# One array of expert rows, one array of attention outputs, and the weight splits on GpSimd

## The chip, the core and the metric

The kernel runs on one core of a Trainium2 chip. The metric is device time in microseconds (us): the median over several executions. One execution was also recorded by the hardware profiler; all rows below come from that one. TensorE is called PE here (its weight loads PEld), VectorE DVE, ScalarE ACT, GpSimd POOL, and SyncE SP, which only issues DMAs.

## The reference

Attention, then a mixture of experts with a skip, then a rational feed-forward layer, all in float32:

```
scores = z @ z.T / S                          # B=8, S=3072, dq=64
x = (u * (relu(scores)**2 @ v)).reshape(24576, 256)
do = x @ w_skip > 0                           # the other tokens keep x
e = argmax(x[do] @ w_gate); g = softmax weight of e     # 8 experts
x[do] += g * (relu(x[do] @ w1[e]) @ w2[e])    # 256 -> 1024 -> 256
h = x @ w_in                                  # 256 -> 2048
P = a0 + a1 h + a2 h^2 + a3 h^3
Q = 1 + |b0| |h| + |b1| h^2
out = (P / (Q + 1e-6)) @ w_out                # 2048 -> 256
```

A float32 matrix is multiplied as a rounded high part and the low rest (`wp` and its second half, `ah` and `al`, `mgh` and `mgl`), so every weight, value and activation has to be split once: a cast makes the high part and a subtraction the low one.

## The kernel before, in words

**Rows, ticks and segments.** The 24576 tokens are 96 attention rows of 256 tokens, 12 rows to a batch. A row is 12 ticks, one for each 256 keys: PE makes the scores `S` of a tick from the transposed keys `T1`, `T4`; ACT and DVE make `ah` and `al` of them; PE adds them times the values `V` into `accA`. Every batch needs its own `T1`, `T4` and `V`, made from loads of `z` and `v` about when the batch begins (the first batch ends with tick 143). The rows are cut into seven segments of 16, 14, 14, 14, 14, 12 and 12 rows (`SEGS`).

**The route of a row** (`r0` to `r21`). When `accA` is complete, DVE multiplies it with `u`, which was loaded into the buffer `xs` (`r0`, L747). SP stores the result into the array of attention outputs (`r21`, L767). PE, ACT, DVE and POOL find expert and gate weight and count the token's place among those of its expert (`r1` to `r14`), POOL turns that into row numbers (`r15`), and POOL scatters 2 x 128 token rows to the 256 slots of their expert in the segment's array `xs{g}` (`r16`, L889), and their numbers into an overflow list `ov` (L895) for tokens that find no slot. Buffer `xs` has two copies, so the load of `u` for row r+2 (L645) waits for the scatters of row r.

**Lag rows.** In all but the last segment, the last `2*LAGT[g]` rows (4, 4, 4, 4, 4, 2) lag: a token of theirs that finds no slot in its own segment may go to the next segment's slots. Since each segment has its array, such a row issues two more scatters (L882, into `xs{g+1}`), and its token number is stored in a mirrored form (`NOTOK`, `MIRROR`), so that the expert stage can tell to which of two output arrays a token belongs.

**The expert stage (MoE1)** of a segment loads 8 tiles of 256 slots (`mr<-xs`, L1191), multiplies them with the expert's weights, four units to a tile (`h`, L1137; `accM`, L1156), and scatters the results back over the attention outputs, `x2_{g}`. In segments 0 to 5 this is four scatters a tile: two of the tokens that belong to `x2_{g}`, two of those of `x2_{g+1}` (`scatter`, L1234). Row numbers out of bounds are dropped. The empty slots were filled with default rows by DMAs of SP (`prefill`, L1418).

**The last layer (MoE2)** then loads the attention outputs of the segment (`mr<-x`, L1191) in tiles of two rows, and its units (`h` at L1148, `accM` at L1166) run mixed with the attention ticks of the next segment.

**Weight preparation.** The expert weights come as raw chunks; the first four are split at their first use, the other 28 by `plan_w1prep`: SP loads two raw halves into `wr` (four buffers), a cast of each half goes into `wp` on ACT, DVE or POOL, a subtraction on DVE or POOL gives the low half, and SP stores the tile to `wsc1`. These chunks are spread over 160 ticks from tick 16. The MoE2 weights are decoded by `plan_w2prep`, nine DVE instructions (L354 to L362) for each half.

**What sets the order.** A planner (`Flow`) is given every piece of work with a wished time and, for each engine that may do it, a duration: "A.52|D.335s|G.588" means ACT at 0.52 us, DVE at 0.335 us or POOL at 0.588 us. It places the pieces one after the other, and the order in which it places them is the program order of each engine's queue. Each engine runs its queue strictly in order. Two DMAs whose declared regions of one DRAM array overlap wait for each other, even where the rows they write differ.

## Time and profile before

| | |
|---|---|
| median of 3 runs | 5580.26 us (5570.92 to 5585.91) |
| the profiled execution | 5576.21 us |
| its span, first to last instruction | 5574.5 us |
| granted TensorE clock, mean over the span | 0.987 |
| busy: PE / PEld / DVE / ACT / POOL | 95% / 90% / 81% / 76% / 58% |

The span begins with attention alone (segment 0, to about 530 us), has the first expert stage to about 690 us, then MoE2 mixed with attention, broken by six more expert stages, to about 5000 us, and MoE2 alone at the end. A time in brackets at the end of a row of the trace is how long the engine had been idle before the instruction, and what it waited for.

### The profile page before, as it was taken

What the parts mean: (1) busy time and instruction counts of PE and PEld (TensorE: products, weight loads), DVE (VectorE), ACT (ScalarE), POOL (GpSimd) and SP (SyncE); (2) the same over time, 40 slices, a digit from 0 to 9 for tenths busy, and PEclk for the clock granted to TensorE, in tenths of its full rate; (3) what the DMA queues carried; (4) which work ended last, traced back from release to release, by engine and by line L of the source; (5) the groups of instructions that cost most, each with busy time, mean ns of one, the idle gap of its engine ahead of it and who ended that gap; (6) DMA issues with size and microseconds to landing.
All of it is one profiled execution on the core that took longest, in us unless ns stands there. A gap on an engine that the chain in (4) does not pass through costs nothing.

```text
span 5574.5 us, 108436 instructions
## 1 busy us (share of the span) xinstructions
PE 5300.9 (95%) x39885; PEld 5026.1 (90%) x39885; DVE 4502.0 (81%) x7499; ACT 4233.4 (76%) x7737; POOL 3259.4 (58%) x4835
## 2 busy tenths in 40 slices
PE   8988899999999999999999999999999999999888
PEld 8988799999999998999999999999998989989777
DVE  6764288884999975999957999949999679986998
ACT  8875388884888874888856888848888668876998
POOL 3434356653655654656545656536566456665998
PEclk9999999999999999999999999999999999999999
DMA  5554521027210046100163101271011540026000
GB/s 191 197 174 145 218 66 56 25 87 258 79 34 29 27 154 233 42 28 23 49 238 139 33 22 59 80 266 55 24 45 39 194 160 29 26 87 211 16 24 17
DMA packets 224816, 540.29 MB, mean 97 GB/s; under 512 B 36978, under 2 KB 136321, under 8 KB 187666
## 3 DMA queue, kind: packets, MB, share of 16 engines
q1 hardware_dynamic: 188754, 448.71, 23.2%
q0 software_dynamic: 35520, 84.56, 4.4%
q8 instruction: 316, 5.18, 0.4%
q14 instruction: 226, 1.85, 0.1%
HBM read 413.38 MB, written 167.41 MB: 104 GB/s over the span
## 4 chain that ended last, share of the span: by engine, by line
PE 61%; DVE 16%; ACT 7%; POOL 6%; issue 6%; DMA 4%; SPq 0%; POOLq 0%; DVEq 0%; ACTq 0%
PE accA L686 21%; PE h L1148 11%; PE accM L1166 11%; PE h L1137 4%; PE accM L1156 4%; PE S L663 3%; PE S L664 3%; DVE mp L1354 2%; DVE h L1355 2%; DVE mq L1369 2%; DVE mgh L1368 2%; DVE al L678 1%; DVE mq L1371 1%; PE lp L777 1%; DMA x<-mo,mti 1%
## 5 line engine op out<-in xcount | busy, mean ns | idle before, releaser
L686 PE MATMUL accA<-V,ah 128*128 128x256 f32 x9216 | 1286.1, 283 | 43.5 <-DVE xs L747 22.3
L1148 PE MATMUL h<-mx,W 128*128 128x512 f32 x4608 | 1212.4, 399 | 43.6 <-DVE mgl L1364 22.3
L686 PEld LDWEIGHTS accA<-V,ah 128*128 128x128 f32 x9216 | 1177.5, 190 | 60.8 <-ACT ah L414 23.9
L410 POOL TENSOR_TENSOR mgl<-mq,mu 128x512 fp32r<-128x512 f32 x496 | 666.5, 1345 | 667.6 <-DVE mq L1371 378.7
L1148 PEld LDWEIGHTS h<-mx,W 128*128 128x128 f32 x4608 | 816.8, 189 | 191.5 <-DVE mgl L1364 26.7
L678 DVE TENSOR_TENSOR al<-S,ah 128x512 fp32r<-128x512 f32 x1152 | 788.2, 685 | 230.4 <-ACT ah L414 198.2
L1166 PE MATMUL accM<-W,mgh 128*128 128x256 f32 x6144 | 849.0, 281 | 19.7 <-DVE mgh L1368 16.9
L667 ACT ACTIVATE S<-S 128x512 f32<-128x512 f32 x1152 | 679.0, 589 | 206.6 <-PE S L664 196.9
L1166 PEld LDWEIGHTS accM<-W,mgh 128*128 128x128 f32 x6144 | 780.7, 189 | 28.7 <-DVE mgh L1368 19.9
L686 PE MATMUL accA<-V,al 128*128 128x256 f32 x4608 | 737.7, 283 | 16.7 <-DVE al L678 16.3
L670 ACT ACTIVATE S<-S 128x512 f32<-128x512 f32 x1152 | 673.7, 585 | 25.0
L1348 POOL TENSOR_SCALAR mq<-mu,coef 128x512 f32<-128x512 f32 x524 | 435.3, 831 | 421.1 <-ACT mu L1341 416.0
L1341 ACT ACTIVATE mu<-h 128x512 f32<-128x512 f32 x768 | 457.7, 596 | 275.2 <-PE h L1148 258.5
L414 ACT ACTIVATE ah<-S 128x512 fp32r<-128x512 f32 x958 | 572.6, 598 | 103.1 <-PE accA L686 72.1
L686 PEld LDWEIGHTS accA<-V,al 128*128 128x128 f32 x4608 | 626.4, 190 | 25.3 <-DVE al L678 21.3
L1354 DVE TENSOR_TENSOR mp<-mp,h 128x512 f32<-128x512 f32 x768 | 521.8, 681 | 122.1 <-ACT mp L1342 113.6
L1342 ACT ACTIVATE mp<-h,coef 128x512 f32<-128x512 f32 x768 | 596.0, 776 | 1.9 <-DVE h L1355 1.6
L664 PE MATMUL S<-T,T 128*128 128x256 f32 x2304 | 591.3, 281 | 0.6 <-ACT T L607 0.4
L1355 DVE SCALAR_TENSOR_TENSOR h<-mp,coef,h 128x512 f32<-128x512 f32 x768 | 573.9, 748 | 3.7
L410 POOL TENSOR_TENSOR mq<-mq,mu 128x512 f32<-128x512 f32 x394 | 520.3, 1322 | 35.0 <-DVE mq L1348 9.4
L1166 PE MATMUL accM<-W,mgl 128*128 128x256 f32 x3072 | 497.4, 284 | 31.4 <-DVE mgl L1364 23.6
L663 PE MATMUL S<-T,T 128*128 128x256 f32 x1920 | 502.1, 286 | 21.6 <-ACT T L588 12.5
(188 smaller groups left out, 9910.0 us busy)
## 6 DMA issues: line engine op xcount, KB each, us to landing
W<-wsc SPq DMA_DIRECT2D x184, 1024.0 KB, 6.2
W<-wsc POOLq DMA_DIRECT2D x48, 1024.0 KB, 5.3
Wv<-wsc SPq DMA_DIRECT2D x64, 512.0 KB, 6.0
vr<-in_v_dram SPq DMA_DIRECT2D x96, 256.0 KB, 2.9
wsc<-wp SPq DMA_DIRECT2D x24, 1024.0 KB, 5.0
xs<-in_u_dram SPq DMA_DIRECT2D x96, 256.0 KB, 2.8
x<-xs SPq DMA_DIRECT2D x96, 256.0 KB, 2.2
mr<-x SPq DMA_DIRECT2D x96, 256.0 KB, 3.3
```

Source lines behind the costliest of these rows:

```text
L410: (nc.vector if e == "D" else nc.gpsimd).tensor_tensor(*a, **k)
L663: mm(o, lhsT=lw, rhs=rw, start=(jj == 0), stop=False, skip_group_check=True)
L664: mm(o, lhsT=lw, rhs=T4[b, ic], start=False, stop=(jj == 1), skip_group_check=True)
L667: act(st["s"], st["s"], AF.Relu, scale=1.0 / S)
L670: act(st["s"], st["s"], AF.Square)
L678: ttt(st["lo"], st["s"], st["hi"].bitcast(F32), op=ALU.subtract)
L686: mm(accs[b, ic][:, it * TT : (it + 1) * TT], lhsT=a[:, jj * TT + it * P : jj * TT + (it + 1) * P], rhs=VV[b, jp][:, vi, jj * D : (jj + 1) ...
L1148: mm(h, lhsT=lw, rhs=rw, start=(k == 0 and i == 0), stop=(k == NK - 1 and i == 2), skip_group_check=True)
L1166: mm(accs_[it // 2][:, it % 2 * TT : (it % 2 + 1) * TT], lhsT=(gh, gl)[part][:, it * P : (it + 1) * P], rhs=w[i][:, 512 + ff * D : 512 + ( ...
L1342: pt("p1", "A.664", ["l1b"], lambda: act(buf("mp"), s["h"], AF.Identity, scale=a3, bias=a2), ["mp"])
L1354: pt("p2", "D.602", ["p1", "abs"], lambda: ttt(s["p"], s["p"], s["h"], op=ALU.mult))
L1355: pt("p3", "D.663", ["p2", "abs"], lambda: stt(s["h"], s["p"], a1, s["h"], op0=ALU.add, op1=ALU.mult), (), ["mp"])
```

## The change

Three things change together. **The arrays:** the seven `xs{g}` become one array with the segments in falling order, and the seven `x2_{g}` one array with the rows in falling order of row pairs. A scatter may write everything below the end of its own segment (`xs[0:xs_end(g)]`, `x2[0:end]`), so it reaches the next segment as well, and the index alone says which: a lag row issues no L882 scatters, an MoE1 tile issues two scatters for four, and the mirrored numbers go. The route's small POOL and DVE instructions of a lag row become fewer (13 to 11 in `r13`, 4 to 2 in `r14`, 7 to 4 in `r15`); those of another row become one more (3 to 4 in `r15`). **The weight splits:** in `plan_w1prep` the subtraction may run on POOL alone, and the cast on POOL or DVE. **The spread:** the 28 chunks are planned over 110 ticks (16 to 126) in place of 160 (16 to 176). Over the whole program the arithmetic on PE is the same; POOL issues 44 scatters into `xs` and 96 into `x2` fewer, and makes 48 weight subtractions (9 before) and 31 weight casts (13 before); DVE makes none of its 39 subtractions and 17 casts (21 before); ACT makes none of its 14 casts. The loop for tokens that overflowed even the next segment gathers from one array; it runs no iteration here.

```diff
@@ declarations
-        xs_d.append(tc.dram_tile([E * TT, RW], F32, name=f"xs{g}"))
-        x2_d.append(tc.dram_tile([(top[g + 1] - top[g]) * TT, D], F32, name=f"x2_{g}"))
+    xs_d = tc.dram_tile([NG * E * TT, RW], F32, name="xs")
+    x2_d = tc.dram_tile([B * S, D], F32, name="x2")
...
+    def xs_end(g):
+        return (NG - g) * E * TT
+
+    def x2_row(row):
+        return B * S - (row // 2 + 1) * 2 * TT
@@ the route
         def r21():
-            nc.sync.dma_start(out=rows4(x2_d[yg], base, ic), in_=R["xs"][:, :, 0:D])
+            nc.sync.dma_start(out=rows4(x2_d, base, ic % 2), in_=R["xs"][:, :, 0:D])
...
             if lag:
-                in2 = R["d"]
-                pool_sel(in2, po, lim, ohf, ALU.is_lt)
-                pool_tt(ovn, ohf, in2, op=ALU.subtract)
-                pool_tt(in2, in2, inn, op=ALU.subtract)
-                pool_tt(R["ex"], loc, in2, op=ALU.mult)
-            else:
-                pool_tt(ovn, ohf, inn, op=ALU.subtract)
+                ts(R["d"], po, scalar1=cap, scalar2=E * TT + cap, op0=ALU.is_ge, op1=ALU.mult)
+                pool_tt(loc, loc, R["d"], op=ALU.subtract)
             pool_tt(loc, loc, inn, op=ALU.mult)
+            pool_tt(ovn, ohf, inn, op=ALU.subtract)
...
-            if i > 3:
+            if i % 2 == 0:
                 nc.gpsimd.indirect_dma_start(
-                    out=xs_d[g + 1][:, :],
-                    out_offset=bass.IndirectOffsetOnAxis(ap=R["ixi"][:, i - 4, 2:3], axis=0),
-                    in_=R["xs"][:, i - 4, :], in_offset=None,
-                    bounds_check=E * TT - 1, oob_is_err=False,
-                )
-            elif i % 2 == 0:
-                nc.gpsimd.indirect_dma_start(
-                    out=xs_d[g][:, :], out_offset=bass.IndirectOffsetOnAxis(ap=R["ixi"][:, t, 0:1], axis=0),
+                    out=xs_d[0 : xs_end(g), :], out_offset=bass.IndirectOffsetOnAxis(ap=R["ixi"][:, t, 0:1], axis=0),
                     in_=R["xs"][:, t, :], in_offset=None,
-                    bounds_check=E * TT - 1, oob_is_err=False,
+                    bounds_check=xs_end(g) - 1, oob_is_err=False,
...
-            (25, 17, "G1.038 Q.37", lambda: r16(4), (16,), lagd, [], []),
-            (26, 18, "G1.038 Q.37", lambda: r16(5), (25, 18), [], [], []),
@@ plan_w1prep
-            add(X(y + 2.0 + 0.3 * half), h, "A.52|D.335s|G.588", lambda e, half=half: hi(e, half), ...
-            add(X(y + 2.4 + 0.6 * half), h + ("l",), "D.602s|G1.245t", lambda e, half=half: lo(e, half), ...
+            add(X(y + 2.0 + 0.3 * half), h, "G.588|D.335s", lambda e, half=half: hi(e, half), ...
+            add(X(y + 2.4 + 0.6 * half), h + ("l",), "G1.245t", lambda e="G", half=half: lo(e, half), ...
@@ the expert stage
-            if both:
-                add(xe + 2.2, k + ("s2",), "G1.038 Q.37", lambda: scatter(0, 1), after=[k + ("s0",)])
-                add(xe + 4.6, k + ("s3",), "G1.038 Q.37", lambda: scatter(1, 1), after=[k + ("s2",)])
...
-                out=x2_d[m.g + i][:, :],
-                out_offset=bass.IndirectOffsetOnAxis(ap=m.ti[h][:, 2 * i + t : 2 * i + t + 1], axis=0),
+                out=x2_d[0:end, :], out_offset=bass.IndirectOffsetOnAxis(ap=m.ti[h][:, t : t + 1], axis=0),
@@ prefill and the plan
-        nc.sync.dma_start(out=xs_d[g][r0 * P : (r0 + 1) * P, :], in_=dflt[:, :])
+        o = xs_end(g + 1) + r0 * P
+        nc.sync.dma_start(out=xs_d[o : o + P, :], in_=dflt[:, :])
...
-        plan_w1prep(c, 16.0 + (c - NW) * (gend[0] - 32.0) / (E * FP1 - NW))
+        plan_w1prep(c, 16.0 + (c - NW) * (TPB - 34.0) / (E * FP1 - NW))
```

The order of the queues changes with the costs that the planner is given. **ACT at the start of the second batch**, before: `S146` are the scores of tick 146, `T1_1_2` the third tile of the second batch's keys, `wp7` the high half of MoE2 weight chunk 7, `xt0_11` and `lg0_11` belong to the route of the first batch's last row.

```order
L588 ACTIVATE T1_1_1_5115<-tp1_1_5114 128x512
L770 ACTIVATE xt0_11_5129<-xp0_11_5128 128x512
L574 ACTIVATE zh1_2_5124<-zr1_2_5122 128x4x64
L1102 ACTIVATE wp7_5178<-wri7_0_5154 128x512
L1102 ACTIVATE wp7_5178<-wri7_1_5181 128x512
L607 ACTIVATE T4_1_1_5059<-t4p1_1_5058 128x256
L784 ACTIVATE lg0_11_5206<-lp0_11_5196 128x18
L667 ACTIVATE S146_5201<-S146_5201 128x512
L670 ACTIVATE S146_5201<-S146_5201 128x512
L588 ACTIVATE T1_1_2_5217<-tp1_2_5216 128x512
```

The same place after the change, from the activations of tick 147 to the next piece of weight preparation:

```order
L670 ACTIVATE S147_5142<-S147_5142 128x512
L673 ACTIVATE S147_5142<-S147_5142 128x512
L411 ACTIVATE ah147_5225<-S147_5142 128x512
L670 ACTIVATE S148_5211<-S148_5211 128x512
L577 ACTIVATE zh1_3_5200<-zr1_3_5198 128x4x64
L673 ACTIVATE S148_5211<-S148_5211 128x512
L610 ACTIVATE T4_1_1_5109<-t4p1_1_5108 128x256
L411 ACTIVATE ah148_5250<-S148_5211 128x512
L670 ACTIVATE S149_5244<-S149_5244 128x512
L673 ACTIVATE S149_5244<-S149_5244 128x512
L591 ACTIVATE T1_1_3_5268<-tp1_3_5267 128x512
L411 ACTIVATE ah149_5288<-S149_5244 128x512
L1079 ACTIVATE wp6_4923<-wri6_1_5124 128x512
```

The two casts of chunk 7 stood ahead of `T4_1_1` and of all scores from tick 146 on; now `T4_1_1` and the scores up to tick 149 stand ahead of the next cast of weights, one of chunk 6.

**DVE at the same place**, before: `cxi7_0` to `wri7_0` is the decoding of chunk 7, `al145` the low activations of tick 145.

```order
L678 TENSOR_TENSOR al145_5152<-S145_5072,ah145_5110 128x512
L354 TENSOR_SCALAR cxi7_0_5155<-wdai7_5013 128x512
L355 SCALAR_TENSOR_TENSOR cxi7_0_5155<-wdai7_5013,cxi7_0_5155 128x512
L578 TENSOR_TENSOR zh1_2_5124<-zr1_2_5122,zh1_2_5124 128x4x64
L356 SCALAR_TENSOR_TENSOR cxi7_0_5155<-wdai7_5013,cxi7_0_5155 128x512
L357 TENSOR_SCALAR wdai7_5013<-wdai7_5013 128x512
L358 TENSOR_SCALAR wdai7_5013<-wdai7_5013 128x512
L359 TENSOR_SCALAR cyi7_0_5156<-cxi7_0_5155 128x512
L360 SCALAR_TENSOR_TENSOR wri7_0_5154<-wdai7_5013,cyi7_0_5156 128x512
L361 TENSOR_TENSOR wri7_0_5154<-wri7_0_5154,cxi7_0_5155 128x512
L362 SCALAR_TENSOR_TENSOR wri7_0_5154<-wdai7_5013,wri7_0_5154 128x512
L1106 TENSOR_TENSOR wp7_5178<-wri7_0_5154,wp7_5178 128x512
```

After, from the low activations of tick 145: the decoding is that of chunk 6, second half, and `V1_8` and `V1_9` are the second batch's values.

```order
L681 TENSOR_TENSOR al145_5194<-S145_5092,ah145_5162 128x512
L355 TENSOR_SCALAR wdbi6_4676<-wdbi6_4676 128x512
L407 TENSOR_TENSOR V1_8_5196<-vr1_8_5106,V1_8_5196 128x512
L356 TENSOR_SCALAR cyi6_1_5126<-cxi6_1_5125 128x512
L681 TENSOR_TENSOR al146_5234<-S146_5099,ah146_5192 128x512
L357 SCALAR_TENSOR_TENSOR wri6_1_5124<-wdbi6_4676,cyi6_1_5126 128x512
L581 TENSOR_TENSOR zh1_3_5200<-zr1_3_5198,zh1_3_5200 128x4x64
L358 TENSOR_TENSOR wri6_1_5124<-wri6_1_5124,cxi6_1_5125 128x512
L681 TENSOR_TENSOR al147_5262<-S147_5142,ah147_5225 128x512
L359 SCALAR_TENSOR_TENSOR wri6_1_5124<-wdbi6_4676,wri6_1_5124 128x512
L407 TENSOR_TENSOR V1_9_5265<-vr1_9_5228,V1_9_5265 128x512
L681 TENSOR_TENSOR al148_5293<-S148_5211,ah148_5250 128x512
```

The decoding and its two subtractions stood in one piece, 20 instructions with one of attention among them, a `zh`; now one instruction of the decoding alternates with one of attention.

**POOL at the scatters of row 14** (buffer `xs14`, `ixi1_2`; a lag row of segment 0), before, from the second scatter into `xs0` (behind `r13` of row 15, which is not shown) to the last into `xs1`; `1_3` is row 15.

```order
L889 DMA xs0_71<-xs14_6698,ixi1_2_7009 2048x258
L882 DMA xs1_73<-xs14_6698,ixi1_2_7009 2048x258
L865 TENSOR_SCALAR ixi1_3_7153<-rix1_3_7145 128x2x2
L867 TENSOR_SCALAR rom1_3_7155<-xs15_6769 128x2
L871 TENSOR_SCALAR rom1_3_7155<-xs15_6769 128x2
L874 TENSOR_SCALAR ixi1_3_7153<-rmx1_3_6916 128x2
L875 TENSOR_SCALAR rsr1_3_7000<-xs15_6769 128x2
L876 TENSOR_TENSOR rsr1_3_7000<-rsr1_3_7000,rm21_3_7020 128x2
L877 TENSOR_TENSOR xs15_6769<-xs15_6769,rsr1_3_7000 128x2
L882 DMA xs1_73<-xs14_6698,ixi1_2_7009 2048x258
```

After, from the first of its scatters into `xs`:

```order
L871 DMA xs_71<-xs14_6675,ixi1_2_6922 14336x258
L743 TENSOR_SCALAR rw1_3_6974<-rd1_3_6953 128x16
L744 TENSOR_TENSOR rw1_3_6974<-rw1_3_6974,rev_102 128x16
L877 DMA ov_73<-rom1_2_6925,ixi1_2_6922 196609x2
L812 TENSOR_TENSOR rd21_3_7008<-rw1_3_6974,rm21_3_6999 128x16
L814 TENSOR_SCALAR rd21_3_7008<-rd21_3_7008 128x16
L815 TENSOR_TENSOR roh1_3_7010<-rd21_3_7008,rcs1_3_6915 128x16
L871 DMA xs_71<-xs14_6675,ixi1_2_6922 14336x258
L821 TENSOR_TENSOR cum1_2_6829<-cum1_2_6829,roh1_3_7010 128x8
L822 TENSOR_TENSOR cum1_3_7045<-cum1_2_6829,roh1_3_7010 128x8
L743 TENSOR_SCALAR rin1_3_7081<-rpo1_3_7073 128x16
L744 TENSOR_TENSOR rin1_3_7081<-rin1_3_7081,roh1_3_7010 128x16
```

The last scatter of row 14 into `xs` stood behind row 15's whole `r13` and `r15`; it now stands ahead of row 15's `r13`.

**SP at the end of the first expert stage**, before: `xs18` and `xs19` are rows of segment 1, `mr8_0` and `mr8_1` the first MoE2 tile.

```order
L1418 DMA xs2_75<-dflt_129 16x2064
L1191 DMA mr7_0_8681<-xs0_71 128x516
L1418 DMA xs2_75<-dflt_129 16x2064
L767 DMA x2_1_74<-xs18_8322 128x2x256
L1191 DMA mr8_0_9221<-x2_0_72 128x2x256
L1191 DMA mr8_1_9223<-x2_0_72 128x2x256
```

After:

```order
L1041 DMA W31_8540<-wsc1_70 128x2048
L1390 DMA xs_71<-dflt_117 16x2064 x2
L1167 DMA mr8_0_9031<-x2_72 128x2x256
L1167 DMA mr8_1_9033<-x2_72 128x2x256
L1390 DMA xs_71<-dflt_117 16x2064
L768 DMA x2_72<-xs18_8267 128x2x256
```

The store of row 18 stood ahead of the first MoE2 loads; it now stands behind them.

## Rows read from the trace of the kernel before

**Rows 1.** Stretches: length, busy time of each engine, granted clock, DMA share, GB/s.

```profile
60.00:320.00 260.00, 245.58 (x2047) 241.51 (x2046) 188.47 (x369) 214.38 (x422) 129.11 (x290) 0.99 0.56 189
320.00:360.00 40.00, 21.76 (x137) 20.38 (x136) 28.07 (x54) 16.36 (x35) 14.72 (x35) 0.71 0.46 155
440.00:520.00 80.00, 59.43 (x463) 58.88 (x462) 27.44 (x64) 46.67 (x92) 45.80 (x126) 0.85 0.24 72
600.00:640.00 40.00, 29.19 (x208) 28.28 (x209) 9.27 (x16) 6.01 (x11) 14.74 (x21) 0.83 0.63 241
680.00:720.00 40.00, 27.52 (x168) 25.06 (x169) 19.93 (x35) 23.59 (x43) 15.82 (x27) 0.83 0.26 86
720.00:5000.00 4280.00, 4166.00 (x31525) 3963.33 (x31524) 3596.09 (x5936) 3290.69 (x6000) 2506.60 (x3752) 0.99 0.25 86
```

**Rows 2.** Waits of PE, 320 to 720 us: total, times, longest.

```profile
PE accA L686 <- DVE xs L747: 20.5, 2, 13.8
PE S L663 <- ACT T L588: 10.6, 2, 10.2
PE mt L1202 <- DMA mr<-x: 8.6, 1, 8.6
PE h L1137 <- DVE mx L1211: 6.5, 2, 6.3
PE mt L1202 <- DMA mr<-xs: 6.1, 3, 3.7
```

**Rows 3.** Timeline of ACT, 338 to 360 us: start, duration, instruction.

```profile
347.96 0.63 ACT L1102 ACTIVATE wp<-wri 128x512 fp32r<-128x512 f32 x1 [4.72 <-DVE wri L362]
354.61 0.63 ACT L1102 ACTIVATE wp<-wri 128x512 fp32r<-128x512 f32 x1 [6.02 <-DVE wri L362]
355.15 0.37 ACT L607 ACTIVATE T<-t4p 128x256 fp32r<-128x256 f32 x1
```

**Rows 4.** Timeline of POOL, 485 to 510 us: three scatters of row 14.

```profile
487.12 1.08 POOL L889 DMA_INDIRECT xs<-xs,ixi  x1 [0.50 <-PE accA L686]
...
495.07 1.06 POOL L889 DMA_INDIRECT xs<-xs,ixi  x1 [0.49 <-issue]
...
499.67 1.04 POOL L882 DMA_INDIRECT xs<-xs,ixi  x1 [0.52 <-issue]
```

**Rows 5.** Timeline of SP's queue, 485 to 510 us: load of `u`.

```profile
502.04 0.37 SPq L645 DMA_DIRECT2D xs<-in_u_dram  x1
```

**Rows 6.** The chain that ended last, 575 to 712 us: start, length, what.

```profile
597.19 7.67 DMA x<-mo,mti
```

**Rows 7.** Timeline of POOL, 660 to 700 us: scatters of the last expert tile.

```profile
661.46 1.04 POOL L1234 DMA_INDIRECT x<-mo,mti  x1 [0.81 <-DVE al L678]
683.20 0.98 POOL L1234 DMA_INDIRECT x<-mo,mti  x1 [20.70 <-DMA x<-xs]
```

**Rows 8.** Timeline of SP's queue, 670 to 700 us.

```profile
680.30 0.37 SPq L767 DMA_DIRECT2D x<-xs  x1
689.95 1.27 SPq L1191 DMA_DIRECT2D mr<-x  x2
```

**Rows 9.** Groups of POOL by form: count, busy us, mean ns, idle before.

```profile
L1234 POOL DMA_INDIRECT x<-mo,mti x208 | 212.2, 1020 | 363.8 <-DMA x<-mo,mti 107.3 <-DVE mo L1226 106.9 <-issue 43.1
...
L851 POOL TENSOR_SCALAR rovl<-rovl 128x16 f32<-128x16 f32 x96 | 25.0, 260 | 8.4
...
L410 POOL TENSOR_TENSOR wp<-wr,wp 128x512 fp32r<-128x512 f32 x9 | 12.3, 1376 | 4.0 <-ACT wp L414 3.8
L418 POOL TENSOR_SCALAR wp<-wr 128x512 fp32r<-128x512 f32 x13 | 9.1, 697 | 47.3 <-DMA wr<-in_moe_w_dram 47.2
```

**Rows 10.** Instructions on tile `wp`: ns min/median/max, first and last start.

```profile
L410 DVE TENSOR_TENSOR wp<-wr,wp x39: 672/684/1737, 46.6 to 403.9; 128x512 fp32r<-128x512 f32 x39
```

**Rows 11.** DMAs by form: issues, KB each, median us to landing.

```profile
xs<-dflt SPq DMA_DIRECT2D x112, 129.0 KB, 4.2
```

**Rows 12.** Waits of POOL, 60 to 320 us: total, times, longest.

```profile
POOL xs L889 <- DMA xs<-xs,ixi: 21.8, 5, 6.4
```

More of the change, by code (lines that the diff above doesn't have):

```diff
@@ L19 @@
 BIG = 1048576.0
-NOTOK, MIRROR = 65536.0, 131072.0
 SEGS = [16, 14, 14, 14, 14, 12, 12]
@@ L250, in tile_attn_moe_moe2 @@
     assert sum(segs) == B * NIC and D == 256 and DQ == 64 and S % 512 == 0
-    assert all(n % 2 == 0 for n in segs) and LAGT[-1] == 0 and 2 * max(segs) * TT < NOTOK
+    assert all(n % 2 == 0 for n in segs) and LAGT[-1] == 0
     nc.scalar.preload_act_table_set("natural_log_exp_and_others")
@@ L426, in tile_attn_moe_moe2 @@
     seg_of = [g for g in range(NG) for _ in range(segs[g])]
-    gtok = [top[g] * TT for g in range(NG)]
+    def xs_end(g):
+        return (NG - g) * E * TT
+    def x2_row(row):
+        return B * S - (row // 2 + 1) * 2 * TT
     def lags(row):
@@ L467, in m_tiles @@
             m.prev = out[-1][0] if out else None
-            m.srcs = [(xs_d, x2_d)[kind - 1][g][(idx * nh + h) * TT : (idx * nh + h + 1) * TT, :] for h in range(nh)]
+            r0 = xs_end(g + 1) + idx * TT if kind == 1 else x2_row(top[g] + 2 * idx)
+            m.srcs = [(xs_d, x2_d)[kind - 1][r0 + h * TT : r0 + (h + 1) * TT, :] for h in range(nh)]
             m.w0 = base + i * FP1 if kind == 1 else base
@@ L730, in plan_route @@
         lag = lags(row)
-        yg = g + lag
-        base = b * S - gtok[yg]
+        base = x2_row(row)
         bc = [P, 2, E]
@@ L907, in plan_route @@
         first = [("pf", g), ("ovp", B - 1)] if row == row0[g] else []
-        if row and lags(row - 1):
-            first = first + old(26)
-        lagd = ([("pf", g + 1)] + (old(26) if lags(row - 1) else [])) if lag else []
+        if lag:
+            first = first + [("pf", g + 1)]
         set_ = row > 0 and (row == row0[g] or (lag and not lags(row - 1)))
@@ L937, in plan_route @@
             (18, 18, "G1.038 Q.37", lambda: r16(2), (16,), [], [], []),
-            (25, 17, "G1.038 Q.37", lambda: r16(4), (16,), lagd, [], []),
-            (26, 18, "G1.038 Q.37", lambda: r16(5), (25, 18), [], [], []),
-            (19, 19, "G1.038 Q.37", lambda: r16(3), (17, 18, 21) + ((26,) if lag else ()), [], [], [("xs", row)]),
-        ):
-            if i in (25, 26) and not lag:
-                continue
+            (19, 19, "G1.038 Q.37", lambda: r16(3), (17, 18, 21), [], [], [("xs", row)]),
+        ):
             add(xl + RT[y], ("rt", row, i), ops, fn, after=[("rt", row, j) for j in dep] + more, takes=tk, frees=fr)
@@ L1185, in plan_half @@
         end = m.nh - 1
-        both = int(m.kind == 1 and LAGT[m.g] > 0)
         def load():
@@ L1271, in plan_half @@
             add(xe + 1.3, k + ("s0",), "G1.038 Q.37", lambda: scatter(0), after=[k + ("p0",), k + ("ti",)] + sc)
-            if both:
-                add(xe + 2.2, k + ("s2",), "G1.038 Q.37", lambda: scatter(0, 1), after=[k + ("s0",)])
-                add(xe + 4.6, k + ("s3",), "G1.038 Q.37", lambda: scatter(1, 1), after=[k + ("s2",)])
             add(
-                xe + (6.0 if both else 4.0), k + ("p1",), "G1.038 Q.37", lambda: scatter(1), after=[k + ("s3" if both else "s0",)],
+                xe + 4.0, k + ("p1",), "G1.038 Q.37", lambda: scatter(1), after=[k + ("s0",)],
                 frees=[("mo", (mi, h)), ("mr", (mi, h)), ("mti", (mi, h))],
```

78 lines of the change are left out of this document (34 added, 44 removed).

## Prediction

> **What bounds the kernel now.** I read the busy times by stretch first [rows 1]. The reader is to see that PE, at 4166 of 4280 us between 720 and 5000 us, is the bound of the mixed stage, where DVE, ACT and POOL all have idle time. So little is to be won or lost there, unless something new stops PE. In four short stretches before 720 us this is not so: PE is idle for 18.2 of 40 us (320 to 360), 20.6 of 80 (440 to 520), 10.8 of 40 (600 to 640) and 12.5 of 40 (680 to 720), 62 us together, and the granted clock falls to 0.71, 0.85, 0.83 and 0.83 in them. Next I read what PE waited for from 320 to 720 us [rows 2]: a few single waits of 6 to 14 us carry most of it. The timelines and the chain then say what each one hangs on [rows 3 to 8]. As the program order is fixed and PE is the bound behind these stretches, a microsecond won there should shift everything behind it.
>
> **The start of the second batch (320 to 360 us).** PE waits 10.2 us for `T` from ACT [rows 2]. ACT itself stood behind two casts of MoE2 weights, which waited 4.7 and 6.0 us for the decoding on DVE; `T4`, next in its queue, ran straight after them [rows 3]. The decoding stood as one block in DVE's queue. In the new order neither is so: the casts stand behind the scores of tick 149, the decoding alternates with attention, and the last expert chunks, which were being split up to 404 us [rows 10], are planned before the switch. The whole idle time of the stretch is 18.2 us; I take 14 of it as gone, since fresh `V` and `zh` still have to be made there, and 4 more for the clock (21.8 us of matmuls at 0.71; at full clock the same work is about 15 us, of which I count two thirds as won): **-18**. Bounds: 0, if the next late piece takes the same place, and -24.
>
> **The lag rows (440 to 520 us).** PE waits 13.8 us in one piece for `xs` of DVE [rows 2]. It is the route's `r0` of row 16, late because the load of `u` began at 502.04 [rows 5], which needed the last scatter of row 14 out of the same buffer, at 499.67 [rows 4]. That scatter into `xs1` no longer exists. The last one into `xs` was at 495.07, and in the new order even this one stands ahead of row 15's `r13`, not behind it. Per lag row POOL saves two scatters of 1.05 us [rows 4] and five small instructions of about 0.26 [rows 9], 3.4 us, which over rows 12 to 15 is near 14 us in a stretch where POOL was busy for 45.8 of 80 [rows 1]. 499.67 to 495.07 is 4.6 us, the 13 instructions of the `r13` that it passes 3.4, and one or two rows' savings before it 3.4 to 6.8: 11 to 15 us earlier, the size of the stall: **-13**. Bounds 0 and -20.5, both waits for `xs` [rows 2]. Against it: the scatters into one array wait for a prefill in flight, 4.2 us to landing [rows 11]; one of row 13's does.
>
> **The first expert stage (600 to 640 us).** PE waits 6.3 us for `mx` of DVE, the chain behind it is a scatter that lands 7.7 us after its start [rows 6], and 6.1 us in three pieces for tiles of `xs`. Four scatters a tile, each behind the one before, become two, so the results' buffer comes free sooner; and SP issues the later tiles' loads earlier among the weight loads. I take **-8** of the stretch's 10.8 idle, since the weight loads themselves (241 GB/s there) may hold some of it. Bounds 0 and -15.
>
> **The end of that stage (680 to 720 us).** PE waits 8.6 us for the first MoE2 tile [rows 2]. A scatter of the last expert tile sat on POOL for 20.7 us [rows 7] until row 18's store, issued at 680.30 [rows 8], had landed, because both wrote `x2_1`; only then could the tile be loaded, at 689.95. In the new order this store stands behind the loads of the tile. Without it the scatters follow the one at 661.46 within some microseconds, and the loads come some 20 us sooner, far more than the 8.6 needed: **-9**, with a little for the clock. Bounds 0 and -12.5.
>
> **The weight splits (60 to 320 us).** Moved to POOL: 39 subtractions at 1.376 us and, in count, 18 casts at 0.697 [rows 9], 53.7 and 12.5 us, 66 us in all, and within 110 ticks in place of 160. POOL was busy for 129 of 260 us [rows 1], so 195 after it. DVE loses 39 x 0.684 [rows 10], about 27 us, and its casts, of 188 busy in 260. What POOL's length hides is its idle time; what would not be hidden is a late scatter, for it holds the `u` load of the row after next. New waits come on top: in the new program order 55 of 192 scatters into `xs` stand behind a prefill issued shortly before, seven of them in the first segment; at 4.2 us to landing [rows 11] these are at most 29 us. That is 224 of 260, near full but not over. The nearest rows on both sides: if the relief of DVE shows on PE (its idle time from 60 to 320 is 14.4 us, part of it waits for DVE), -10; if all of POOL's present gaps stayed, 131 + 129 + 95 = 355 us for 260, +95. The gaps are waits for other engines in an ordered queue and shrink when the queue is behind; only the waits for scatters to land (21.8 us [rows 12]) must stay, which makes 246 of 260. Nearest to the lower end: **+6**.
>
> **Mixed stages.** Gone are some 80 scatters of MoE1 at 1.02 us [rows 9] and those of 18 lag rows; POOL has 1773 idle us there [rows 1]. The prefill waits lie beside the same idle time: 48 at 4.2 us are 202 us at the most. Without this cover they would come out at full length. I take **0**, bounds -10 and +10.
>
> **The sum.** -18 - 13 - 8 - 9 + 6 = -42. The profiled execution took 5576.21 us, 4 us under the median of the three runs: 5534.
>
> The Trainium skill speaks against the move: "SBUF — State Buffer", section "Who interferes with whom", says that a VectorE instruction with two SBUF inputs and a GpSimd instruction that reads SBUF exclude each other for the whole instruction of whichever came first. This trace agrees as far as it goes: the DVE subtraction into `wp` took 684 ns in the median and 1737 at the longest [rows 10], 1.05 us more, which is within one POOL subtraction. By the rule every subtraction that moves may hold DVE; the rival below prices that from rows.
>
> **Rivals.**
> First: **DVE is held up by POOL's subtractions.** The longest DVE subtraction is 1.05 us over its median [rows 10]. Were each of the 39 that moved to cost DVE its full length, 39 x 1.376 = 54 us against 27 relieved, DVE would be at about 215 of 260 and late for `al` here and there. I price that at +20 in place of +6: 5548. For it speaks the maximum; against it that the median, 684, is next to the minimum, 672, with 22 splits on POOL already. Chance 0.12.
>
> Second: **the waits only move.** Behind a stall that is gone the next comes due: the weight loads of the expert stage, `V` of the new batch, the buffers `xs` with two copies. If three quarters of the 48 us come back, -12 + 6 = -6: 5570. For it speaks that the four stretches follow each other closely; against it that between them PE is not waiting, and that the first three have separate causes. Chance 0.15.
>
> Third, on the other side: **POOL becomes the bound of the first batch.** The route's chain goes to and fro between POOL, PE, ACT and DVE, and each return finds POOL inside a subtraction of 1.376. Then a row's scatters fall behind, the `u` load of two rows later too, and PE waits in every row from 60 to 320 us; SP's queue stands behind raw buffers that POOL has not freed, with loads of `u` behind them. It turns the result when POOL costs more than 48 + 17 = 65 us, that is when two thirds of the 95 us above come out; at 80 the time is 5608. For it: 246 of 260 us leaves almost nothing. Against it: none of PE's waits there is for POOL's scatters now. Chance 0.1.
>
> Not a rival: that the change does nothing; the new order shows the fewer scatters and the moved work.
>
> **How the numbers follow.** The likeliest case, 5534, has 0.6, with a range of its own of 5515 to 5555. About 0.3% (17 us) is what a measurement of this kernel can tell from no change. The first rival is also faster, the second is mostly within 0.3%, the third slower; 0.03 is left for anything else, above all for less or more in the mixed stages. Faster 0.75, same 0.15, slower 0.1. At the bottom the range goes to the four gains at their bounds (-24 - 20.5 - 15 - 12.5 = -72, and 0 for POOL, which gives 5504), cut to 5508 because all four at once is unlikely; at the top it takes in the second rival with some loss in the mixed stages, 5578.
>
> **What would show it.** Right: no wait of PE above 5 us at 340 to 360 us; the wait for `xs` at about 490 gone; no POOL scatter of some 20 us wait before the first MoE2 tile; PE at 95% again right behind; POOL at about 195 to 225 of the first 60 to 320 us with PE no more idle than 25 us there. Wrong: PE waiting for `xs` in several rows before 320 us (third rival), DVE's `al` much over 685 ns in the mean there (first), or the same 10 us waits at other lines before 720 us (second).

## The result

The changed kernel takes 5500.65 us in the median of four runs (5489.75 to 5504.8) against 5579.7 before: a ratio of 0.9856, with a 95% interval of 0.9837 to 0.9876. That is 79 us less, where 46 were forecast, and 7 us below the lower end of the range. Run again beside other versions, it took 5497.62, a ratio of 0.9845 (0.9832 to 0.9858). The profiled execution has a span of 5500.5 us, 74 under the one before, with the clock at 0.992 in the mean (0.987 before).

First the stretches of the changed kernel that answer to [rows 1]. Columns: from and to, length, busy time (and count) of PE, PEld, DVE, ACT and POOL, granted clock, DMA share, GB/s.

```profile
60.00:320.00 260.00, 240.08 (x1941) 235.24 (x1940) 173.05 (x323) 196.94 (x386) 179.29 (x340) 0.97 0.66 223
320.00:360.00 40.00, 39.09 (x330) 38.19 (x329) 34.92 (x66) 33.60 (x68) 27.31 (x47) 1.00 0.39 122
430.00:660.00 230.00, 211.84 (x1738) 208.55 (x1737) 104.55 (x195) 124.37 (x235) 84.09 (x200) 0.98 0.61 224
646.00:4924.00 4278.00, 4177.20 (x31634) 3976.42 (x31633) 3596.37 (x5890) 3290.01 (x6003) 2439.29 (x3642) 1.00 0.25 87
```

The stretch before that holds the same matmuls as 430 to 660 us (to six) is this one:

```profile
440.00:720.00 280.00, 225.37 (x1744) 218.51 (x1743) 104.05 (x200) 127.12 (x241) 116.19 (x263) 0.91 0.50 184
```

The reader is to see two things in this pair. PE's idle time falls from 54.6 to 18.2 us, by 36; and its busy time, for the same work, falls from 225.4 to 211.8, by 13.5, with the clock at 0.98 in place of 0.91. So these 230 us took 50 less than before, not the 30 of my three terms. The start of the second batch runs without a stop: 0.9 us idle of 40, clock 1.00. From 60 to 320 us PE has 5.5 us more idle time and the clock is at 0.97 in place of 0.99; PE does 106 matmuls fewer than before (1941 against 2047 [rows 1]), some 13 us of work at 0.12 us each. POOL has 179 us of work there.

Next the longest waits of PE from 320 to 720 us, against [rows 2] (total, times, longest):

```profile
PE mt L1178 <- DMA mr<-xs: 8.2, 3, 4.0
PE accA L689 <- DVE xs L749: 2.9, 1, 2.9
PE accA L689 <- DVE al L681: 2.4, 5, 1.0
```

The waits of 13.8, 10.2, 8.6 and 6.3 us are gone; of the old list the loads of expert tiles are left, and 2.9 of 20.5 us for `xs`. Single rows of the timelines show why. On ACT, the next cast of MoE2 weights now runs behind the second batch's `T4` (L610), where two of them stood right ahead of it [rows 3]:

```profile
349.85 0.37 ACT L610 ACTIVATE T<-t4p 128x256 fp32r<-128x256 f32 x1
352.66 0.64 ACT L1079 ACTIVATE wp<-wri 128x512 fp32r<-128x512 f32 x1
```

On SP's queue, the load of `u` for row 16 begins at 473.05 us, against 502.04 [rows 5]; it is 29 us earlier, of which some 10 had been won before this place:

```profile
473.05 0.46 SPq L648 DMA_DIRECT2D xs<-in_u_dram  x1
```

At the end of the first expert stage POOL's scatters no longer wait 20.7 us for a store of row 18 [rows 7]: the last one waits 3.3 us. The loads of the first MoE2 tile begin 6.5 us before PE uses it, and the store follows them (against [rows 8]):

```profile
623.83 0.97 POOL L1210 DMA_INDIRECT x<-mo,mti  x1 [3.27 <-DMA x<-mo,mti]
...
626.39 1.26 SPq L1167 DMA_DIRECT2D mr<-x  x2
...
632.89 0.60 PE L1178 MATMUL mt<-ident_r,mr 128*128 128x128 f32 x4
...
639.43 0.38 SPq L768 DMA_DIRECT2D x<-xs  x1
```

To compare whole programs, take the ticks as milestones: the first activation of each tick (`S`, L667 before, L670 after) stands once in ACT's records, 1152 of them, and its start is when tick n (counted from 0) got there. The table gives these starts before, in us from the first instruction, and how much earlier (-) or later (+) the other kernels are. Tick 264 lies behind the first expert stage; 1151 is the last tick.

| tick | before, us | changed | e1 splits | e2 arrays | e3 spread | e5 no pair | e6 no lag scatters | e9 decoding | e10 arrays, decoding | e11 pair apart |
|---|---|---|---|---|---|---|---|---|---|---|
| 120 | 274.1 | +7.6 | -0.8 | +1.2 | +13.4 | +3.3 | +1.3 | -5.9 | +4.0 | +3.1 |
| 132 | 298.2 | +15.8 | +0.8 | +1.2 | +13.8 | +3.3 | +1.3 | +1.5 | +7.4 | +3.1 |
| 168 | 403.4 | -9.9 | -6.7 | -2.6 | -8.0 | +3.2 | +1.1 | -11.5 | -5.3 | +2.8 |
| 216 | 639.3 | -32.7 | -9.8 | -24.5 | -29.0 | -1.9 | -8.6 | -12.1 | -25.0 | -2.3 |
| 264 | 816.1 | -60.4 | -9.9 | -52.2 | -56.7 | -27.4 | -7.0 | -12.3 | -52.7 | -11.7 |
| 720 | 2776.9 | -73.2 | -10.1 | -69.0 | -67.7 | -41.0 | -8.8 | -15.2 | -70.0 | -15.8 |
| 1151 | 4939.0 | -77.1 | -6.3 | -81.3 | -77.4 | -61.4 | -5.8 | -13.5 | -83.8 | -15.0 |

Two profiles of the changed kernel itself differ by up to 5 us in these places, so nothing below that is read. The changed kernel: 8 us lost by tick 120 and 16 by tick 132, 26 won from there to tick 168, 50 between ticks 168 and 264, and 17 more up to the last tick, where I had 0.

### The profile page after: what moved, and what is told of

The parts are those of the page before. It is cut to its first block, busy times and chain, and to the rows that moved or that the text cites. A ratio compares the mean times of both kernels' runs of the same rounds, so it can differ in the third digit from the quotient of the medians.

```text
span 5500.5 us, 107941 instructions
## 1 busy us (share of the span) xinstructions
PE 5288.3 (96%) x39885; PEld 5018.9 (91%) x39885; DVE 4479.5 (81%) x7383; ACT 4210.9 (77%) x7695; POOL 3224.2 (59%) x4725
## 4 chain that ended last, share of the span: by engine, by line
PE 65%; DVE 13%; ACT 7%; POOL 6%; issue 5%; DMA 4%; SPq 0%; DVEq 0%; POOLq 0%; ACTq 0%
PE accA L689 21%; PE h L1125 12%; PE accM L1143 12%; PE accM L1133 5%; PE h L1114 5%; PE S L666 3%; PE S L667 3%; DVE mq L1340 2%; DVE mp L1325 2%; DVE h L1326 2%; DVE mgh L1339 1%; DVE al L681 1%; POOL mq L407 1%; PE lp L778 1%; DMA vr<-in_v_dram 1%
## 5 line engine op out<-in xcount | busy, mean ns | idle before, releaser
L670 ACT ACTIVATE S<-S 128x512 f32<-128x512 f32 x1152 | 678.9, 589 | 195.8 <-PE S L667 180.3
L1319 POOL TENSOR_SCALAR mq<-mu,coef 128x512 f32<-128x512 f32 x557 | 457.3, 821 | 450.1 <-ACT mu L1312 443.9
L411 ACT ACTIVATE ah<-S 128x512 fp32r<-128x512 f32 x940 | 561.3, 597 | 80.2 <-PE accA L689 47.7
L667 PE MATMUL S<-T,T 128*128 128x256 f32 x2304 | 590.7, 280 | 0.1
L407 POOL TENSOR_TENSOR mq<-mq,mu 128x512 f32<-128x512 f32 x419 | 555.7, 1328 | 40.9 <-ACT mq L1317 11.8
L1143 PE MATMUL accM<-W,mgl 128*128 128x256 f32 x3072 | 497.2, 284 | 33.0 <-DVE mgl L1335 24.5
```

The lines of the kernel that those rows point to most:

```text
L407: (nc.vector if e == "D" else nc.gpsimd).tensor_tensor(*a, **k)
L667: mm(o, lhsT=lw, rhs=T4[b, ic], start=False, stop=(jj == 1), skip_group_check=True)
L670: act(st["s"], st["s"], AF.Relu, scale=1.0 / S)
L1143: mm(accs_[it // 2][:, it % 2 * TT : (it % 2 + 1) * TT], lhsT=(gh, gl)[part][:, it * P : (it + 1) * P], rhs=w[i][:, 512 + ff * D : 512 + ( ...
```

## The experiments

### The two halves of the change

**e1** puts the new splits and their spread into the kernel before; **e2** takes them out of the changed one; **e3** leaves only the spread:

```diff
# e1, on the kernel before (e2: the reverse, on the changed kernel; e3: e2 but the last line)
-            "A.52|D.335s|G.588" ... "D.602s|G1.245t"
+            "G.588|D.335s" ... "G1.245t"
-        plan_w1prep(c, 16.0 + (c - NW) * (gend[0] - 32.0) / (E * FP1 - NW))
+        plan_w1prep(c, 16.0 + (c - NW) * (TPB - 34.0) / (E * FP1 - NW))
```

e1: 

> The kernel before with the weight splits and their spread of the change, and the old arrays. Theory (the parts act at places of their own and add): the stop of about 10 us of PE at the second batch is gone, the first batch costs some 6 us more, the stalls of the lag rows and of the first expert stage (13.8, 6.3, 8.6 us) stay: 5570 us, 8 to 15 under the kernel before. Rival (the gain belongs to the new order as a whole, whatever part sets it off): at least 30 under.

Measured: 5573.93 us, ratio 0.9985 (0.9974 to 0.9995).

e2: 

> The changed kernel with the old weight splits (ACT, DVE or POOL, 160 ticks). Theory (parts add): the stalls of the lag rows and of the first expert stage are gone, the 10 us stop at the second batch is there: 5512 us, 60 to 70 under the kernel before. Rival (the order as a whole): less than 50 under, because the early stop spoils what follows.

Measured: 5499.05, ratio 0.9855 (0.9838 to 0.9871).

e3: 

> The changed kernel with the splits free to run on ACT, DVE or POOL as before, but spread over 110 ticks as in the change. If the 7 us that the first batch lost are POOL's doing: 7 us under the changed kernel, 5494, with POOL busy for about 140 of 60 to 320 us. If they are the denser spread's doing whatever the engine: as the changed kernel within 4 us. If ACT and DVE are too full for the denser spread: up to 15 us over it.

Measured: 5500.98, ratio 0.9856 (0.9839 to 0.9872).

At tick 264 the halves add as the theory has it: -9.9 and -52.2 against -60.4 together. At the end they do not: -6.3 and -81.3 are 10 us more than the change's -77.1, and in the median the arrays alone are as fast as the whole change. So the move of the splits to GpSimd and the denser spread are worth some 10 us on the old arrays, and nothing that can be measured on the new ones. e3 says the same: with the splits free to go anywhere the time is the changed kernel's within 1 us.

Nor do they add in the first batch: at tick 132 they are at +0.8 and +1.2, the change at +15.8. e1's expectation of 6 us there did not come true, though POOL does the splits in it; e3, where POOL does no more than before, is 13.8 us behind. These are e1 and then e3 from 60 to 320 us (columns as in the first fence):

```profile
60.00:320.00 260.00, 246.38 (x2052) 243.17 (x2052) 188.29 (x339) 207.97 (x412) 184.29 (x344) 0.99 0.67 228
60.00:320.00 260.00, 239.49 (x1961) 234.15 (x1960) 186.98 (x375) 211.39 (x415) 132.51 (x290) 0.98 0.66 227
```

With 184 us of POOL's work PE does as many matmuls as in the kernel before (2047 [rows 1]), with 133 us it does 86 fewer. So what the first batch loses is not lost to POOL's work. By e3's alternatives it goes with the denser spread; e1 has that too, and loses nothing on the old arrays.

In e2 the stop at the second batch is still there, as PE's longest waits from 320 to 720 us show:

```profile
PE S L666 <- ACT T L591: 13.1, 3, 11.6
PE mt L1178 <- DMA mr<-xs: 8.5, 3, 3.7
PE accA L689 <- DVE xs L749: 2.9, 1, 2.9
```

### What stopped PE at the second batch

**e9** changes one line of the kernel before, the spread of the MoE2 chunks; **e10** the same line of e2:

```diff
-        plan_w2prep(fp, 14.0 + fp * (gend[0] - 40.0) / FP2)
+        plan_w2prep(fp, 14.0 + fp * (TPB - 34.0) / FP2)
```

e9: 

> The kernel before with the eight MoE2 chunks decoded over 110 ticks (14 to 124) in place of 152, so that no block of decoding stands at the second batch; weight splits and arrays as before. If that block made the stop at 347 to 357 us: the 10 us wait for T is gone, the stretch from tick 132 to 168 takes 15 to 20 us less, 8 to 18 under the kernel before at the end. If the expert chunks still being split there are to blame: the wait stays at over 5 us.

Measured: 5568.2, ratio 0.9983 (0.9973 to 0.9993). In the trace no wait for `T` is left among the longest from 320 to 720 us, and the others of [rows 2] stand:

```profile
PE accA L686 <- DVE xs L747: 19.9, 2, 13.6
PE mt L1202 <- DMA mr<-x: 8.8, 1, 8.8
PE accA L686 <- ACT ah L414: 8.5, 6, 2.5
PE mt L1202 <- DMA mr<-xs: 5.9, 2, 3.5
PE h L1137 <- DVE mx L1211: 5.2, 1, 5.2
```

This shows that the decoding of MoE2 weights made the stop. It is not the only way to be rid of it: in e1, which plans the decoding as before and moves the splits, the wait for `T` is gone from the list too, with a wait for `zh` of 5.6 us in its place. From tick 132 to 168 e9 gains 13 us (+1.5 to -11.5), a little under what was expected.

e10: 

> The one-array kernel with the old weight splits and the decoding over 110 ticks: what the two parts give without moving a split to GpSimd. If gains at separate places add: 5485 to 5495, some 5 to 15 under the changed kernel, with no stop over 5 us at the second batch. If a denser first batch takes it back, as with the spread of the splits: within 4 us of the changed kernel.

Measured: 5494.21 (5487.74 to 5497.3), ratio 0.9849 (0.983 to 0.9867). It is the lowest median of all versions, without one split moved. It beats the kernel before. The changed kernel's two medians are 3 and 6 us above it, but the intervals overlap, so these runs do not separate the two.

### What the second pair of scatters cost

**e5** leaves the pair out of the kernel before (`if both:` becomes `if False:`, and the last scatter of a tile is wished 2 us sooner); the expert results of lag tokens are lost. The planner orders it anew. **e11** keeps the pair, in the same order on every engine, but sends it to arrays of its own, so that nothing waits for it and it waits for no store; the same results are lost:

```diff
# e11
-                out=x2_d[m.g + i][:, :],
+                out=(x2n_d if i else x2_d)[m.g + i][:, :],
```

e5: 

> The kernel before without the second pair of scatters of an expert tile (into the next segment's outputs); the expert results of lag tokens are left out. Theory (the ends of the expert stages, the false wait for row 18's store among them, and the clock that falls with them): PE's waits of 8.6 and 6.3 us in the first stage go, the one of 13.8 us stays; 25 us under the kernel before by the end of the first stage and 35 to 45 at the end of the run. Rival (most of the gain is the lag rows'): under 20.

Measured: 5513.06, ratio 0.9867 (0.9851 to 0.9884).

e11: 

> The kernel before in the same order, but the second pair of scatters of an expert tile goes to arrays of its own, which nothing else reads or writes; the expert results of lag tokens are lost. So the scatters stay and only their waits for row stores, and of the loads for them, go. If the false wait for the store of row 18 made the stop of 8.6 us: that stop is gone, 9 to 13 us under the kernel before by tick 240, the 6.3 us wait for mx stays, and at the end 10 to 25 under. If the count of scatters is what makes the stage late: no gain beyond 5 us by tick 240.

Measured: 5569.79, ratio 0.9983 (0.9973 to 0.9993).

Longest waits of PE, 320 to 720 us, of e5 and then of e11:

```profile
PE accA L686 <- DVE xs L747: 20.7, 2, 13.8
PE S L663 <- ACT T L588: 9.9, 1, 9.9
PE mt L1202 <- DMA mr<-xs: 7.9, 2, 7.0
```

```profile
PE accA L687 <- DVE xs L748: 19.8, 2, 13.7
PE S L664 <- ACT T L589: 10.7, 2, 10.2
PE mt L1203 <- DMA mr<-xs: 6.6, 2, 3.8
```

In both the 8.6 us for the first MoE2 tile has gone from the list, so the false wait for row 18's store made that stop, as the prediction said; it is worth 12 us by tick 264 and 15 at the end, clock included. In e11 the 6.3 us for `mx` went as well, which I had expected to stay. But most of what e5 wins is neither: e5 is at -27.4 by tick 264 and at -61.4 at the end, the largest single part of the whole change, and 34 of it come later, nearly all over the five later expert stages (6.1 us from tick 384 to 408, 9.4 from 576 to 600, 5.2 from 720 to 744, 7.3 from 888 to 936, 4.7 from 1056 to 1104). My expectation for e5 (35 to 45) was too low. What PE waits for in these stages can be read in part: with the pair it waits for tiles of `xs`, whose buffers come free with the last scatter of an earlier tile. From 820 to 4960 us, of the kernel before, of e11 and of e15 (below):

```profile
PE mt L1202 <- DMA mr<-xs: 12.7, 5, 3.6
PE mt L1203 <- DMA mr<-xs: 10.2, 4, 3.3
PE mt L1179 <- DMA mr<-xs: 14.7, 6, 3.7
```

In e5 and in the changed kernel no such wait is left there. The rest of the 34 us is not traced to a wait.

**e4** and **e15** put the pair back into the changed kernel, in segments 0 to 5, with the same rows written a second time: e4 into the same array, e15 into one of its own. Both are planned anew, and have the same order on every engine.

```diff
# e4; in e15 s2 and s3 write an array x2n that nothing else uses; in both, p1 is wished 2 us later, behind s3
+                add(xe + 2.2, k + ("s2",), "G1.038 Q.37", lambda: scatter(0), after=[k + ("s0",)])
+                add(xe + 4.6, k + ("s3",), "G1.038 Q.37", lambda: scatter(1), after=[k + ("s2",)])
```

e4: 

> The changed kernel with four scatters to a tile of the expert stage again in segments 0 to 5; the second pair writes the same rows a second time, so nothing else differs. If the count of scatters in a row made the later tiles late: 15 to 35 us over the changed kernel, with waits for mx or mr<-xs of some 6 us again in the first stage and 2 to 4 in the later ones. If it was the waits between different arrays (the store of row 18 ahead of a scatter): within 8 us of the changed kernel.

Measured: 5665.95, ratio to the kernel before 1.0148 (1.0132 to 1.0165): 165 us over the changed kernel.

e15: 

> The changed kernel with the second pair of scatters of an expert tile again in segments 0 to 5, into an array of its own which nothing else uses: the count is back, without waits for stores and without four landings in a row. If the count is what made the stages late, in the changed kernel as in the one before: 12 to 18 us later by tick 264 and 35 to 50 at the end. If the pair's cost lay in the waits between arrays: under 8 us at the end. Against 165 us for the same pair in one array.

Measured: 5555.97, ratio to the kernel before 0.995 (0.9935 to 0.9965): 55 over the changed kernel; 25 later by tick 264 and 58 at the last tick, both over what I expected (12 to 18 and 35 to 50).

Waits of POOL's scatters over the whole run, of the changed kernel, of e4 and of e15:

```profile
POOL x L1210 <- DMA x<-mo,mti: 124.6, 37, 7.3
```

```profile
POOL x L1210 <- DMA x<-mo,mti: 331.9, 116, 6.1
...
POOL x L1210 <- DMA x<-xs: 35.1, 6, 9.2
```

```profile
POOL x2n L1211 <- DMA x2n<-mo,mti: 82.4, 23, 6.8
...
POOL x L1211 <- DMA x<-mo,mti: 51.8, 19, 6.0
```

In one array each scatter waits until the one before has landed, and four landings in a row cost 110 us more than two pairs that overlap; as e4 and e15 have one order, this is the array's doing. Even where they overlap, the pair with its order costs 58 us at the last tick in the new kernel (e15), as it costs 61 in the old (e5). How much of either is the new order of the queues, these two cannot say; that both come out alike speaks for the pair. e4 missed its range by far, because it did not test the count alone: it made the chain of landings twice as long as either kernel has it.

### The lag rows

**e6** takes the two L882 scatters out of the kernel before (lag tokens without a slot in their own segment get no expert); **e12** adds to the changed kernel, in unchanged order, as many small instructions to a lag row as the change took out:

```diff
# e6
-            if i in (25, 26) and not lag:
+            if i in (25, 26):
# e12: two more in r13, two reductions in r14, three in r15, all repeats; one of them:
-            pool_tt(ovl, po, eovf, op=ALU.add)
+            for _ in range(3 if lag else 1):
+                pool_tt(ovl, po, eovf, op=ALU.add)
```

e6: 

> The kernel before without the two extra scatters of a lag row; its small instructions stay, and the lag tokens that find no slot in their own segment get no expert. Theory: the 13.8 us wait for xs before tick 204 goes or falls below 6 us, 10 to 20 us under the kernel before by the end of the first stage, and the waits of 8.6 and 6.3 us stay. Rival (the small instructions of the route are what made row 14 late): the wait stays over 8 us.

Measured: 5576.43, ratio 0.9986 (0.9976 to 0.9996). The wait for `xs` in the lag rows falls from 13.8 to 8.1 us, just over the 8 at which the rival was to hold:

```profile
PE accA L686 <- DVE xs L747: 11.5, 2, 8.1
PE mt L1200 <- DMA mr<-x: 10.8, 1, 10.8
```

e12: 

> The changed kernel in the same order, with five small POOL instructions and two small DVE reductions more in the route of each lag row (repeats of ones that are there), as many as the change took out. If the small instructions were what made row 14's buffer late beside the two scatters: the wait for xs of row 16 grows from 2.9 to 7 to 9 us, and the time by tick 240 by 5 to 8 us. If it was the order (the last scatter ahead of row 15's r13): the wait stays under 5 us, and the time within 4 us.

Measured: 5522.76 (5518.5 to 5526.71), ratio to the kernel before 0.9895 (0.9874 to 0.9917): 22 us over the changed kernel. From 430 to 720 us:

```profile
PE mt L1181 <- DMA mr<-xs: 7.2, 3, 3.7
PE accA L689 <- DVE xs L749: 6.9, 2, 4.0
```

The extra scatters were one part of the long wait, and the small instructions another: with them back, the waits for `xs` go from 2.9 to 6.9 us and tick 264 comes 7.5 us later. What I had not priced is that they cost 12 us more later: 20 at the last tick, for 22 lag rows, with jumps near the ends of the segments. On POOL these are instructions of about 0.26 us [rows 9], on an engine that is busy for 59% of the span.

**e13** asked whether the same holds for one instruction of every row: e10 with both index columns out of one instruction again.

> The one-array kernel with the old splits and the early decoding, and one small POOL instruction less in the route of every row: both index columns come out of one instruction, as in the kernel before. Seven small instructions more in a lag row cost the changed kernel 20 us over 22 rows, 0.13 us for each. If these lie on the path that frees the buffer of the row: 3 to 12 us under the version without it (5494), at 5482 to 5491. If the planner's new order weighs more than one instruction: 5490 to 5505.

Measured: 5513.07 (5498.53 to 5515.94), ratio 0.9875 (0.986 to 0.989), above e10 and, beside it on the same chip, above the changed kernel:

> The changed kernel itself, beside the others on the same chip: 5497 to 5503. A version is called better only where its runs lie below these.

Measured (**e14**): 5497.62. So the small gain, if there is one, did not show. That it was lost in the order that the planner made with the new cost is likely, as little else differs, but not shown. The theory that every instruction of the route pays is not borne out here.

### What a stop of PE costs

**e7** and **e8** stop PE in the changed kernel by sending the low activations of some ticks to DRAM and back before PE reads them:

```diff
# e7; in e8 n % 24 == 6 and range(1)
+            if 264 <= n < 1128 and n % 72 == 6:
+                for _ in range(3):
+                    nc.sync.dma_start(out=trip.bitcast(F32)[:, :], in_=st["lo"].bitcast(F32))
+                    nc.sync.dma_start(out=st["lo"].bitcast(F32), in_=trip.bitcast(F32)[:, :])
```

e7: 

> The changed kernel with 12 stops of PE put into the stages from tick 264 on: the low activations of one tick in 72 go to DRAM and back three times. If a long stop costs its idle time and a stretch at the lower clock behind it: the time grows by 1.2 to 1.5 times the idle time that is added to PE, with stretches at half clock behind most of the stops. If a stop costs what it lasts: 1.0 times. I expect 8 to 15 us of idle a stop and 120 to 240 us in all.

e8: 

> As the run with the long stops, but one round trip at one tick in 24, 36 stops of about a third of the length: PE's added idle time is near that of the other run or less, the clock stays up, and the time grows by 1.0 to 1.1 times the added idle time. If the clock falls in short stops as well: as the other run.

Measured: 5656.24 and 5571.13, 156 and 70 over the changed kernel. The first lines of the pages of the changed kernel, of e7 and of e8, the last two each followed by the wait that was put in (total, times, longest):

```profile
span 5500.5 us, 107941 instructions
...
PE 5288.3 (96%) x39885; PEld 5018.9 (91%) x39885; DVE 4479.5 (81%) x7383; ACT 4210.9 (77%) x7695; POOL 3224.2 (59%) x4725
```

```profile
span 5661.1 us, 108041 instructions
...
PE 5318.0 (94%) x39885; PEld 5045.4 (89%) x39885; DVE 4479.3 (79%) x7383; ACT 4210.5 (74%) x7695; POOL 3222.5 (57%) x4725
```

```profile
PE accA L694 <- DMA al<-trip: 136.1, 12, 16.2
```

```profile
span 5572.4 us, 108049 instructions
...
PE 5314.8 (95%) x39885; PEld 5040.2 (90%) x39885; DVE 4485.0 (80%) x7383; ACT 4213.5 (76%) x7695; POOL 3228.4 (58%) x4725
```

```profile
PE accA L694 <- DMA al<-trip: 50.5, 24, 5.0
```

Of the 36 short stops 24 show as waits of PE. The count of matmuls is the same in all three, but PE is busy for 29.7 us longer with 12 long stops and 26.5 with 36 short ones, while its idle time (span less busy) grows by 130.9 and 45.4. The span grows by 1.23 and 1.58 times the idle time. The mean clock is 0.992, 0.978 and 0.987. So a stop does cost more than it lasts: e7 is within what was expected of it, but the short ones are not spared, as I had expected them to be. Per microsecond of idle time they cost more, by one profile of each.

## Why the prediction was wrong

The direction held, and all of the named mechanisms but that of the weight splits; the sum was too small by 33 us. By its own terms:

- **The start of the second batch, -18.** Right in place, too small in size: PE's 18.2 us of idle time there went to 0.9 and the clock from 0.71 to 1.00, and from tick 132 to 168 the kernel won 26 us. e9 shows the cause.
- **The weight splits, +6.** Near the number at tick 120 (+7.6), but not at tick 132 (+15.8), and not by the mechanism that I gave: e1 has the splits on POOL and loses nothing (+0.8 at tick 132), e3 has them off it and loses nearly as much (+13.8). The loss is there where a denser first batch meets the one array (the change, e3 and, with 7.4 us, e10) and not on the old arrays (e1, e9); why, stays open. This term and the one before miss by 8 to 10 us each, in opposite directions. That together they come to -10 where -12 was forecast is luck. POOL was busy for 179 us in that stretch against my 195; 8 of the difference lay before 60 us (19.1 us of POOL there, against 11.0). The text ahead of the prediction speaks of 28 chunks; its count of 48 subtractions and the kernel (`range(NW, E * FP1)`, 8 to 31) have 24. The sum went by the counts, so this does not touch it.
- **The first rival** left a trace, at a small price. The mean of `al` on DVE, which I had named as its sign, was 686 ns in that stretch in both kernels, but `al` is no test. One of its two inputs, the scores `S`, lies in PSUM, and the rule of the Trainium skill ("SBUF — State Buffer", section "Who interferes with whom") is about VectorE instructions with both in SBUF. The subtraction into `wp` has both there, and this trace agrees with the rule: one took 2875 ns, with 682 in the median. It began inside the first of two POOL subtractions in a row and ended 0.6 us after the second, as the two rows below show. Added up over DVE's groups from 60 to 320 us, the time above a group's median is about 10 us before and 20 after; the rival had priced 54. DVE's busy time fell from 188 to 173 us, and PE's waits for `al` from 5.8 to 3.3.

```profile
93.92 2.88 DVE L1083 TENSOR_TENSOR wp<-wri,wp 128x512 fp32r<-128x512 f32 x1
...
93.70 2.54 POOL L407 TENSOR_TENSOR wp<-wr,wp 128x512 fp32r<-128x512 f32 x2
```

- **The third rival,** a bound POOL, is out: POOL had 81 us to spare. Its sign is there in small: from 60 to 320 us PE waits 6.2 us in four places for `xs` (2.3 in three before), and 4.3 us for POOL's counts (0.6 before).
- **The lag rows, -13, and the first expert stage with its end, -8 and -9.** The stops named were the right ones, and all went. The step that failed is the price: I took each term as a part of the idle time of its own stretch, and counted the clock for the second batch (two thirds of what it took) and nearly not at all here. The three terms make 30, the trace has 50: 36 of idle time and 13.5 of matmuls that ran at the lower clock. Counted in matmuls on PE, the 3200th, 3600th, 4500th and 5000th, which began at 438, 511, 643 and 725 us before, begin 9.9, 29.5, 38.5 and 58.5 us earlier. So the lag rows gave 20 us for 13, the expert stage 9 for 8, and its end 20 for 9. That a stop costs more than its length, with a lower clock, is also what e7 and e8 show: 0.23 and 0.58 us more for each microsecond of idle time.
- **Mixed stages, 0 with bounds of 10.** Wrong by 17. I argued from POOL's 1773 idle microseconds that the scatters taken out there were covered. As a mean over 4280 us this is true, but the cost lies at the five later expert stages, where PE waits for tiles whose buffers the scatters hold: e5, without the pair, wins 34 us there, and the lag rows' small instructions cost 12 more in e12. The parts alone sum to more than the change has: at the last tick 6 (e1), 61 (e5), 6 (e6) and 20 (e12) make 93, against 77; at tick 264 they make 52 against 60. The planner deals the order anew in e1, e5 and e6; e13, 15 us above the changed kernel with one instruction fewer in a row, suggests that this alone can move the time by some 10 us. What of the missing 16 us is order and what is the new waits of the one array (POOL waited 28.1 us in seven places for prefills) stays open; no version was run in which a scatter declares a smaller region.
- **The second rival,** that the waits only move, did not come about. Three quarters of the gain would have had to return; the gain grew instead.

## What to carry to other kernels

Idle time of a helper engine over a whole stage says little about a chain of it that others wait for: look at what its last link frees, at the place where the stage turns over, and price it there. Where the main engine stands still, add to the stop what its clock loses; here that was a quarter to more than a half again. And when a change has several parts, run each alone: one of these two halves, the moved splits, was worth nothing measurable beside the other.

## What the runs showed of the hardware

Scatters whose declared regions overlapped followed each other by a landing, not by an issue: with four in one array to a tile the waits for landings rose from 124.6 to 331.9 us and the run by 165 us; in the same order, with two pairs in two arrays, the run rose by 55. A DVE subtraction with both inputs in SBUF that began inside a POOL subtraction took 2.88 us in place of 0.68, while `al`, with one input in PSUM, never took more than 0.70 beside the same POOL work up to 320 us. And stops of PE of at most 5 us lowered the clock (0.987 in the mean against 0.992), at 1.58 us of run for each microsecond of idle time.
